# Linear attention and a routed feed-forward layer on one core: constant products beside the keys, products of quarters for the queries, routing in three groups of twelve

## The chip, the cores and the metric

The kernel runs on one core of a Trainium2 chip. The metric is the device time of one execution in microseconds (us). Three runs of the kernel before took 615.9, 616.95 and 619.54 us; their median, 616.95 us, is the time before. All times inside the kernel come from one further execution that the hardware profiler recorded.

The core's engines are TensorE (PE in the profile, with its weight loads as PEld), VectorE (DVE), ScalarE (ACT), GpSimd (POOL) and SyncE (SP, which here only issues DMAs). Each works through its own list of instructions in order and waits for others by semaphores.

## The reference

Eight sequences of 576 tokens with 8 heads of 64 go through linear attention and a norm, and then every one of the 4608 tokens goes through the one expert of eight that it scores highest.

```python
kv = np.einsum('bhsd,bhse->bhde', k, v)
out = np.einsum('bhsd,bhde->bhse', q, kv)
rms = np.sqrt(np.mean(out * out, axis=-1, keepdims=True) + 1e-06)
x = (out / rms * g_norm)            # then rows: 4608 x 512
logits = x @ w_gate
e_idx = np.argmax(logits, axis=1)
gate_w = softmax(logits)[token, e_idx]
eom = 1.0 / (1.0 + np.exp(-(x @ w_output_gate)))
for e in range(8):
    h = np.maximum(x[mask] @ w1[e], 0.0)        # 512 -> 1024
    out[mask] = gate_w * eom[:, e] * (h @ w2[e])  # 1024 -> 512
```

## The kernel before

**Phase one, attention and routing** (`p1_main`, line 837). The loop runs over the 8 sequences, called batches here. For each, `kv_part` (line 460) multiplies keys by values: four chunks of 128 tokens (s = 0 to 3) and a rest of 64 (s = 4), eight products per chunk (line 474; the profile counts two records for each product of 32-bit numbers). ACT copies the sums into `aug` (line 480), DVE into `kvc` (line 482). `kvT_part` (line 485) transposes them and `m_part` (line 494) multiplies them by the gate weights, so that each query row later gives 64 values and 16 gate scores per head.

`out_tile` (line 515) then treats 128 tokens, 36 tiles in all: products of queries with `aug` (line 541, tile `ops`), and three ACT operations that take the result out of PSUM (lines 546, 548, 549). Two PSUM buffers of the tag "big" serve `ops` and the sums of `m_part` in turn. One tile later, DVE adds up the squares (line 562, tile `ss`). During batch b the tiles of batch b-1 are made, the calls of `run_out` (line 797) put them between the steps. Most tiles lie in one batch and multiply 64 rows by 128 tokens at a time; the four tiles across two batches multiply by 64 tokens at a time.

**Routing** (`route`, line 572) is a generator that treats a group of tiles at once with some thirty small DVE operations: the norm's root (lines 589 to 611), the scaling of the gate scores (`gp`, line 618), their sums (`lg`, line 622), the choice of the expert (`ohb`, line 648), a prefix sum on PE (`rps`, lines 676 to 683), the place of each token in its expert's list (lines 689 to 699), one-hot matrices `la` (lines 710 to 723, on the engines that `PLACES` names) and `rrc` (lines 729 to 736), and a table product on PE (`tblps`, line 749). It stops at each `pause`; `advance` (line 787) takes it on to the next one. After the group that ends with tile 23 (`LEAD_GROUP`), the expert with the most tokens so far is known, and its first 384 rows, called the lead here, are worked on before the other tiles are routed.

**The order** in phase one is the program's own (`manual_schedule`, engines in `MAN`): what is written first stands first in each engine's list. `HOOKS` names steps after given tiles and `TAIL` the steps after the last one: R advances the routing, L takes the lead one step on (`lead_run`, line 368: split of the first weights, the three tiles' `stage`, then `mm1`, f = 0 to 7), S splits a chunk of the second weights (`lead_w2`), G gathers the lead's rows, W loads the second weights.

**Slots**: 30 buffers of 4 KB per partition (`SLOTS`) hold loads, rows, weights and so on. `load` (line 448) issues loads as long as more than `SPARE` are free.

**Phase two** (line 1013) runs over nine runs: run 0 is the lead, run 1 the same expert's other rows (320), and then seven experts. `mm1` (line 287) multiplies the rows by the first weights, in eight blocks f of 12 or more products (line 308, tile `hps`, in the two "big" buffers), which ACT and DVE take out (lines 317 and 318, `hT`). `mm2` (line 327) multiplies by the second weights (lines 345 and 350, `yps`), and the rows go out by an indirect DMA (line 361). `stage` (line 255) scales the gathered rows by the norm's root (on DVE or POOL, as `NORMS` says), transposes them on PE (line 271, `tps`) and splits them into a high and a low part on ACT and DVE (lines 276 and 277, `xT`). Weights are split in the same way (`split`, line 198; `whi`, `wlo`). In run 0 the rest of the lead's `mm1`, its three `mm2` and the `stage` steps of run 1 are woven together.

## Time and profile before

| what | value |
|---|---|
| median of three runs | 616.95 us |
| the profiled execution | 620.81 us |
| span of its instructions | 618.8 us |
| TensorE products busy | 566.5 us (92%) |
| DVE, ACT, POOL busy | 263.2, 222.0, 164.0 us |
| granted TensorE clock, mean | 0.931 of full |
| read from and written to memory | 72.63 and 19.99 MB |

The span runs from the first to the last instruction; the execution's 620.81 us contain 2 us more around it. The view by windows gives, for a stretch, the busy time and number of instructions of PE, PEld, DVE, ACT and POOL, then the granted TensorE clock (1.00 is full), the share of the DMA engines in use and the data rate in GB/s. The timeline gives start, length, engine, line, operation, tiles and shapes, and in brackets the idle time before and what ended it; times overlap where an engine is pipelined, so that the distance of two starts is the price of an operation. A shape such as 64*128 64x80 is the part of TensorE's array in use (rows*columns) and the moving operand.

### The profile page before, as it was taken

The page shows a single profiled execution, that of the slowest core. Times are in us where ns is not written, and L with a number is a line of the kernel's source. Part 1 is how long each engine was busy: PE and PEld are TensorE (multiplying, and loading weights), DVE is VectorE, ACT ScalarE, POOL GpSimd, SP SyncE. Part 2 cuts the span into 40 slices and gives each one's busy share as a digit, 9 for nine tenths or more (in the row PEclk, how much of TensorE's full clock was granted, in tenths as well). Part 3 has the DMA queues.
Part 4 walks back from the last instruction along what each step waited for, and adds up shares of the span by engine and source line. Part 5 has one row for each costly group of instructions (what it writes and reads, how often), then busy time and mean ns, then how long its engine had stood idle before and what let it go on. Part 6 is the DMA issues. An engine that isn't in the chain of part 4 may idle for free.

```text
span 618.8 us, 10459 instructions
## 1 busy us (share of the span) xinstructions
PE 566.5 (92%) x4179; PEld 506.3 (82%) x4179; DVE 263.2 (43%) x536; ACT 222.0 (36%) x413; POOL 164.0 (27%) x163
## 2 busy tenths in 40 slices
PE   3799978848999999999899999999999999999991
PEld 3688868747898998889789988998799889889881
DVE  2123688699425456225331453235135325424300
ACT  1335545634225334323331343234234423523310
POOL 2001044443832510630036117104500630110010
PEclk9958777579999999999999999999999999999996
DMA  8999991770564622349776332524432451110010
GB/s 271 367 409 407 405 366 49 246 285 7 166 231 138 202 89 90 87 169 35 16 159 199 115 122 91 172 69 138 145 112 74 135 181 68 53 52 2 0 47 14
DMA packets 39122, 92.53 MB, mean 150 GB/s; under 512 B 14418, under 2 KB 14546, under 8 KB 39072
## 3 DMA queue, kind: packets, MB, share of 16 engines
q1 hardware_dynamic: 32176, 71.63, 37.4%
q0 software_dynamic: 6464, 20.00, 10.2%
q8 instruction: 34, 0.56, 0.4%
q10 hardware_dynamic: 432, 0.21, 0.1%
q14 instruction: 16, 0.13, 0.1%
HBM read 72.63 MB, written 19.99 MB: 150 GB/s over the span
## 4 chain that ended last, share of the span: by engine, by line
PE 57%; issue 19%; DMA 10%; DVE 4%; POOL 3%; ACT 3%; another core or an unknown queue 2%; SPq 0%; POOLq 0%; DVEq 0%
PE hps L308 24%; PE yps L350 23%; PE ops L541 3%; PE kvps L474 3%; DMA ld<-kvm 3%; DMA xs<-xrow 2%; PE tps L271 2%; POOL out L361 2%; DMA ld<-qT 2%; DMA ld<-rem 2%; PE yps L345 1%; POOL xg L239 1%; DMA wraw<-w 1%; DMA xg<-xs,gidx 1%
## 5 line engine op out<-in xcount | busy, mean ns | idle before, releaser
L308 PE MATMUL hps<-xT,whi 128*128 128x320 f32 (+4 forms) x1024 | 197.3, 310 | 9.5 <-DVE hT L318 8.4
L350 PE MATMUL yps<-whi,hT 128*128 128x512 f32 (+2 forms) x592 | 195.9, 399 | 1.0 <-ACT whi L221 1.0
L308 PEld LDWEIGHTS hps<-xT,whi 128*128 128x128 f32 x1024 | 163.6, 191 | 11.9 <-DVE hT L318 9.1
L350 PEld LDWEIGHTS yps<-whi,hT 128*128 128x128 f32 (+2 forms) x592 | 111.3, 188 | 25.2 <-ACT whi L221 1.2
L308 PE MATMUL hps<-xT,wlo 128*128 128x320 f32 (+4 forms) x512 | 121.6, 309 | 0.0
L318 DVE SCALAR_TENSOR_TENSOR hT<-hps,hT 128x512 fp32r<-128x512 f32 (+5 forms) x112 | 59.2, 529 | 142.6 <-ACT hT L317 142.3
L350 PE MATMUL yps<-wlo,hT 128*128 128x512 f32 (+2 forms) x296 | 116.6, 394 | 0.8 <-DVE wlo L224 0.8
L317 ACT ACTIVATE hT<-hps 128x512 fp32r<-128x512 f32 (+5 forms) x112 | 52.5, 469 | 164.0 <-PE hps L308 121.6
L308 PEld LDWEIGHTS hps<-xT,wlo 128*128 128x128 f32 x512 | 89.0, 191 | 0.0
L361 POOL DMA_INDIRECT out<-y,oidx x42 | 44.8, 1068 | 154.2 <-ACT y L360 107.2
L239 POOL DMA_INDIRECT xg<-xs,gidx x42 | 43.2, 1029 | 137.5 <-PE tps L271 54.6
L350 PEld LDWEIGHTS yps<-wlo,hT 128*128 128x128 f32 (+2 forms) x296 | 55.7, 188 | 12.1 <-DVE wlo L224 1.1
L217 DVE SCALAR_TENSOR_TENSOR wlo<-wraw,gcol,whi 128x1024 fp32r<-128x1024 f32 x32 | 43.9, 1372 | 39.6 <-ACT whi L214 39.6
L247 POOL TENSOR_TENSOR xg<-xg 128x512 f32<-128x512 f32 (+3 forms) x40 | 44.0, 1102 | 43.9 <-DMA xg<-xs,gidx 43.5
L541 PE MATMUL ops<-aug,ld 64*128 64x80 f32 (+1 forms) x640 | 49.0, 327 | 5.8 <-ACT gp L549 5.7
L541 PEld LDWEIGHTS ops<-aug,ld 64*128 64x128 f32 (+1 forms) x640 | 44.5, 230 | 8.8 <-ACT gp L549 6.4
L360 ACT ACTIVATE y<-yps,tl 128x512 f32<-128x512 f32 (+2 forms) x37 | 25.5, 689 | 71.4 <-PE yps L350 68.4
L276 ACT CAST xT<-tps 128x512 fp32r<-128x512 f32 (+3 forms) x45 | 23.6, 530 | 67.6 <-PE tps L271 63.9
L277 DVE TENSOR_TENSOR xT<-tps,xT 128x512 fp32r<-128x512 f32 (+3 forms) x45 | 27.7, 617 | 46.9 <-ACT xT L276 43.3
L474 PE MATMUL kvps<-ld 128*64 128x64 f32 (+1 forms) x640 | 36.4, 300 | 11.1 <-DMA ld<-kvm 10.7
L474 PEld LDWEIGHTS kvps<-ld 128*64 128x64 f32 (+1 forms) x640 | 33.1, 209 | 14.0 <-DMA ld<-kvm 12.0
L224 DVE TENSOR_TENSOR wlo<-wraw,whi 128x1024 fp32r<-128x1024 f32 x28 | 34.3, 1226 | 13.5 <-ACT whi L221 6.7
(158 smaller groups left out, 403.2 us busy)
## 6 DMA issues: line engine op xcount, KB each, us to landing
wraw<-w SPq DMA_DIRECT2D x64, 512.0 KB, 3.2
ld<-kvm SPq DMA_DIRECT2D x32, 512.0 KB, 10.2
ld<-qT SPq DMA_DIRECT2D x18, 512.0 KB, 10.2
xs<-xrow SPq DMA_DIRECT2D x13, 512.0 KB, 10.4
xs<-xrow SPq DMA_DIRECT2D x2, 1280.0 KB, 15.2
ld<-rem SPq DMA_DIRECT2D x3, 512.0 KB, 10.2
xg<-xs,gidx POOLq DMA_INDIRECT x42
out<-y,oidx POOLq DMA_INDIRECT x42
```

Source lines behind the costliest of these rows:

```text
L217: eng.scalar_tensor_tensor(out=lo, in0=r, scalar=gcol[:, 0:1], in1=hi.bitcast(F32), op0=ALU.mult, op1=ALU.subtract)
L224: eng.tensor_tensor(out=lo, in0=r, in1=hi.bitcast(F32), op=ALU.subtract)
L239: nc.gpsimd.indirect_dma_start(out=x[:M, :], out_offset=None, in_=rows, in_offset=bass.IndirectOffsetOnAxis(ap=gidx[:M, p, t:t + 1], axis=0))
L247: eng.tensor_tensor(out=v, in0=v, in1=f, op=ALU.mult)
L277: nc.vector.tensor_tensor(out=lo[:, :, c0:c0 + M], in0=v, in1=hi.bitcast(F32)[:, :, c0:c0 + M], op=ALU.subtract)
L308: nc.tensor.matmul(ps[:, j, :n], w[:, o:o + P], x[d][:, j * N:j * N + n], start=(d == 0 and k == 0), stop=(d == 3 and k == 2))
L317: nc.scalar.activation(hh, x, AF.Relu)
L318: nc.vector.scalar_tensor_tensor(out=v(h[:, l:l + n]), in0=x, scalar=0.0, in1=hh.bitcast(F32), op0=ALU.max, op1=ALU.subtract)
L350: nc.tensor.matmul(ps[:M], a, b, start=(f == 0 and k == 0), stop=(f == 7 and k == 2))
L361: i_ = nc.gpsimd.indirect_dma_start(out=out, out_offset=bass.IndirectOffsetOnAxis(ap=oidx[:M, p, t:t + 1], axis=0), in_=y[:M], in_offset=N ...
L474: nc.tensor.matmul(ps[u * D:(u + 1) * D, p * D:(p + 1) * D], k, v, start=(s == 0 and p == 0), stop=(s == 4 and p == NP - 1))
L541: nc.tensor.matmul(ps[r0:r0 + m, u, p * W:(p + 1) * W], qt[g // 2][r, p, q0:q0 + m], augs[b % 3][r, p, :], start=True, stop=True)
```

## The change

**Groups.** `GR` becomes (12, 12, 12): three groups, of which the second ends with tile 23. The first group's gate scores are scaled on DVE (`GPSIMD_GROUPS` 0), its `la` all made on POOL, the second group's on POOL and DVE in turn, the third's on POOL, ACT and DVE in turn. In the second and third group `lg` is summed in two halves (`APART`). Every pause is one stop (`WAITS` is gone).

**Constants.** `constant` multiplies a tile of ones by itself into PSUM that nobody reads, 256 columns for 64 outputs: three products ahead of each of a batch's four chunks, 20 more before the first, and 56 in the tail (step C).

**Steps.** `kv_part` stops before s = 2 and before s = 4, and a tile is made at each stop.

**Quarters.** `out_tile` multiplies 64 rows by 64 tokens in every tile, so that a tile has 16 products instead of 8.

**The lead.** Its rows are scaled on DVE. Its gather and the loads of its weights come after tile 29 instead of after tile 30 and in the tail. In the tail the third group's routing comes first, and the lead's `mm1` and `mm2` (step Y) follow before phase two, whose run 0 now holds only the gather and the `stage` of run 1.

**Slots.** 13 of the 30 are kept for rows (`xfree`), 17 are left for loads; `SPARE` is gone. SP joins the engines whose order is the program's.

```diff
-GR = (10, 10, 4, 12)
+GR = (12, 12, 12)
...
+ROWS = LEAD_TILES // 2 + 1
...
-TAIL = "QLLLLRRRSLSRRSLLRRRLSLRRSRLSLL"
+HOOKS = {25: 'R', 26: 'R', 27: 'R', 28: 'R', 29: 'R', 30: 'RGXW'}
+TAIL = "Q" + 7 * "RC" + "LLLL" + 3 * "RL" + "SLSLSLSLLL" + "YYY"
+COLD = (3, 20)
+GPSIMD_GROUPS = 0
+APART = (1, 2)
...
-NORMS = ("PPP", "VPVP")
-PLACES = ['P', 'P', 'PAV', 'PAV', 'PAV']
+NORMS = ("VVV", "VPVP")
+PLACES = ['P', 'PV', 'PAV']
...
+    def constant(ps, n, start):
+        for _ in range(n):
+            nc.tensor.matmul(ps[0:D, 256:512], ones[:, 0:D], ones.unsqueeze(1).to_broadcast([P, 2, P]), start=start, stop=start)
...
         for s in range(5):
+            if s in (2, 4):
+                yield
+            if s < 4:
+                constant(ps, COLD[0] + (COLD[1] if b == 0 and s == 0 else 0), s == 0)
...
-                for u in range(2):
-                    r = slice(u * D, (u + 1) * D)
-                    nc.tensor.matmul(ps[r0:r0 + m, u, p * W:(p + 1) * W], qt[g // 2][r, p, q0:q0 + m],
-                                     augs[b % 3][r, p, :], start=True, stop=True)
+                for c0 in range(r0, r0 + m, D):
+                    q0 = g % 2 * P + c0
+                    for u in range(2):
+                        r = slice(u * D, (u + 1) * D)
+                        nc.tensor.matmul(ps[c0:c0 + D, u, p * W:(p + 1) * W], qt[g // 2][r, p, q0:q0 + D],
+                                         augs[b % 3][r, p, :], start=True, stop=True)
...
+        elif step == "C":
+            constant(ps_t.tile([P, 512], F32, name="cps", tag="t"), 8, True)
+        elif step == "Y":
+            mm2(0, state["y"], {})
+            state["y"] += 1
...
             if i == 0:
                 gather(1)
                 scale_rows(1)
-                for _ in lead:
-                    next(lead2, None)
-                for _ in lead2:
-                    pass
+                for h in hT[0]:
+                    give(h)
+                for x in range(len(tiles_of(1))):
+                    stage(1, x)
+                continue
```

The first place to see it is TensorE's list in the batch numbered 3 (`aug_117` holds the sums of batch 2, `ld` a load). Before:

```order
L474 MATMUL kvps<-ld 64x64 x40
L541 MATMUL ops<-aug_117,ld 128x80 x8
L489 MATMUL kvTps<-ident,kvc 128x128 x2
L541 MATMUL ops<-aug_117,ld 128x80 x16
L501 MATMUL mps<-gw,kvT 64x16 x8
```

Now, from the second pair of chunks on:

```order
L468 MATMUL kvps<-ones 64x256
L488 MATMUL kvps<-ld 64x64 x8
L556 MATMUL ops<-aug_117,ld 64x80 x16
L488 MATMUL kvps<-ld 64x64 x8
L556 MATMUL ops<-aug_117,ld 64x80 x16
L503 MATMUL kvTps<-ident,kvc 128x128 x2
```

The keys' products stand in pieces between tiles, the constants ahead of them, and each tile has twice the products of half the width. The second place is TensorE's list behind the last tile (`tps`: the lead's transposes, `hps`: its first products, `tblps`: the third group's table). Before:

```order
L541 MATMUL ops<-aug_116,ld 128x80 x32
L271 MATMUL tps<-ident,xg 128x128 x12
L308 MATMUL hps<-xT,whi 128x384 x2
L308 MATMUL hps<-xT,wlo 128x384
L308 MATMUL hps<-xT,whi 128x384 x2
```

Now, after the last of the third group's prefix products:

```order
L697 MATMUL rps<-ohb_118,triu 128x104
L468 LDWEIGHTS ones
L468 MATMUL cps<-ones 64x256
...
L274 MATMUL tps<-ident,xg 128x128 x12
L763 LDWEIGHTS la
L763 MATMUL tblps<-rrc,la 128x96
...
L311 MATMUL hps<-xT,whi 128x384 x2
```

The lead's first products used to follow its transposes at once; now the third group's prefix products stand before the transposes, and its table product between them and `hps`. The third place is DVE's list from the last sums of squares on. Before:

```order
L562 TENSOR_REDUCE ss<-sq 128x8 x3
L267 COPY tl<-xg 128x1
L277 TENSOR_TENSOR xT<-tps,xT 128x2x128 x2
...
L217 SCALAR_TENSOR_TENSOR wlo<-wraw,gcol,whi 128x1024
L589 TENSOR_SCALAR ra<-ss 128x96
...
L618 TENSOR_TENSOR gp<-gp,xtail 128x1536
L318 SCALAR_TENSOR_TENSOR hT<-hps,hT 128x384
```

Now:

```order
L577 TENSOR_REDUCE ss<-sq 128x8 x7
L603 TENSOR_SCALAR ra<-ss 128x96
...
L687 TENSOR_SCALAR rogs<-rogs 128x12
L219 TENSOR_SCALAR whi<-wraw,gcol 128x1024
L220 SCALAR_TENSOR_TENSOR wlo<-wraw,gcol,whi 128x1024
L250 TENSOR_TENSOR xg<-xg 128x512
L270 COPY tl<-xg 128x1
L280 TENSOR_TENSOR xT<-tps,xT 128x2x128 x2
...
L703 TENSOR_TENSOR rw<-rps,ohb_118 128x96
```

The routing of the third group up to `rogs` has moved ahead of the lead's first weights and rows, and the rest of it, from `rw` on, stands directly behind them and ahead of the lead's first `hT`.

More of the change, by code (lines that the diff above doesn't have):

```diff
@@ L165, in body, with take @@
     ps_y = main.enter_context(tc.tile_pool(name="ps_y", bufs=1, space=psum))
[L166 removed]
+    free = list(range(SLOTS - ROWS))
+    xfree = list(range(SLOTS - ROWS, SLOTS))
     held = {}
[L169 removed]
+    def take(shape, dt, name, free=free):
         i = free.pop(0)
@@ L332, in mm2 @@
         T = half(i)
-        ps = ps_y.tile([P, DM], F32, name="yps", tag=f"y{ny % 2}")
-        ny += 1
+        if i == 0:
+            ps = ps_b.tile([P, 2, 512], F32, name="yps0", tag="big")[:, 0]
+        else:
+            ps = ps_y.tile([P, DM], F32, name="yps", tag=f"y{ny % 2}")
+            ny += 1
         tl = tails.pop((p, t))
@@ L352, in mm2 @@
                 e()
-        y = hp.tile([P, DM], F32, name="y", bufs=3)
+        y = take([P, DM], F32, "y0") if i == 0 else hp.tile([P, DM], F32, name="y", bufs=3)
         if M == T:
@@ L446, in body, with load @@
                 nq += 1
-    def load(spare):
-        while loads and len(free) > spare:
+    def load():
+        while loads and free:
             where, k, src = loads.pop(0)
@@ L804, in run_out @@
             advance()
-            load(SPARE)
+            load()
             if not loads and not opened[0]:
                 open_rows(0)
-            if lead_placed and opened[0] and (0, 1, 0) not in raw and (1, 0) not in wgt:
-                for c in range(1):
-                    wload(0, 1, c)
             for step in HOOKS.get(done_tiles, ""):
@@ L855, in p1_main @@
             advance()
+        for _ in lead:
+            assert False
+        for _ in lead2:
+            assert False
     vec = nc.vector
```

59 lines of the change are left out of this document (26 added, 33 removed).

## The prediction

> **What bounds the kernel now.** I read the page first, then the busy times by windows, then the timelines of PE and DVE from the first loads to the second run.
>
> ```profile
> span 618.8 us, 10459 instructions
> 28.00:48.00 20.00, 16.95 (x228) 15.31 (x230) 3.76 (x6) 8.23 (x21) 0.00 (x0) 0.50 1.03 409
> 48.00:84.00 36.00, 32.14 (x612) 29.45 (x610) 20.25 (x59) 18.50 (x51) 8.87 (x11) 0.80 1.03 402
> 84.00:118.00 34.00, 28.25 (x400) 26.07 (x393) 29.86 (x97) 18.88 (x52) 13.91 (x19) 0.68 0.55 170
> 118.00:175.00 57.00, 44.29 (x222) 38.14 (x221) 39.29 (x90) 19.80 (x40) 29.89 (x26) 0.86 0.53 173
> 174.69 0.45 PE L308 MATMUL hps<-xT,whi 128*128 128x320 f32 x2
> 161.93 5.48 PE yps L350 x24
> ```
>
> Up to 84 us the loads run at full rate (DMA share 1.03, some 405 GB/s), but PE is behind them, at 0.50 to 0.80 of its clock. From 84 to 118 us the DMA share halves and DVE is the fullest engine (29.86 of 34 us): it routes. From 118 to 175 us PE has 57 us for the lead. The first product of run 1 starts at 174.69; from there on the order of work is the same in both kernels, and PE works nearly without a gap. So what the change is worth is how far 174.69 moves. I split the time before it at two marks: A, DVE's copy `kvc` of batch 6, and B, the end of the last tile's products.
>
> ```profile
> 28.69 1.12 PE L474 MATMUL kvps<-ld 128*64 128x64 f32 x16 [0.73 <-DMA ld<-kvm]
> 60.66 0.42 DVE L482 COPY kvc<-kvps 128x256 f32<-128x256 f32 x1 [4.27 <-ACT aug L480]
> 84.14 0.42 DVE L482 COPY kvc<-kvps 128x256 f32<-128x256 f32 x1 [1.88 <-ACT aug L480]
> 109.02 8.65 PE L541 MATMUL ops<-aug,ld 64*64 64x80 f32 x96
> 137.04 1.01 PE L308 MATMUL hps<-xT,whi 128*128 128x384 f32 x2 [7.76 <-DVE hT L318]
> ```
>
> A is at 84.14, B at 109.02 + 8.65 = 117.67. Between B and run 1 lie 57.0 us; one stall of 7.76 us in them is PE waiting for DVE, which had the routing in front of `hT`.
>
> **Up to A: quarters, steps, constants, slots.** The rows for prices at half and at full clock:
>
> ```profile
> 35.62 1.30 PE L541 MATMUL ops<-aug,ld 64*64 64x80 f32 x30
> 83.52 0.72 PE L541 MATMUL ops<-aug,ld 64*64 64x80 f32 x30
> 46.15 3.81 PE L474 MATMUL kvps<-ld 128*64 128x64 f32 x80
> 95.53 4.58 PE L474 MATMUL kvps<-ld 128*64 128x64 f32 x80
> 112.00:116.00 4.00, 4.00 (x40) 3.81 (x38) 2.74 (x4) 2.74 (x7) 3.36 (x5) 0.50 0.70 190
> 124.00 0.84 PE L308 MATMUL hps<-xT,whi 128*128 128x384 f32 x2
> 124.96 0.84 PE L308 MATMUL hps<-xT,whi 128*128 128x384 f32 x2
> 127.53 0.52 PE L308 MATMUL hps<-xT,whi 128*128 128x384 f32 x2
> 128.07 0.52 PE L308 MATMUL hps<-xT,whi 128*128 128x384 f32 x2
> 77.06 6.50 POOL L719 TENSOR_SCALAR la<-ni,rlon 128x128 bf16<-128x128 f32 x10 [18.75 <-DVE rlon L698]
> ```
>
> Quarters are in the trace: the tiles across two batches have them. Such a tile (32 records, 30 of them in the row) costs 1.4 us cold and 0.8 warm. The 8.65 us hold one such tile and four of the other kind, all cold: (8.65 - 1.4) / 4 = 1.8 each. The gain is 0.4 us for each of 32 tiles when cold, some 13 us of PE time.
>
> A constant product has no row. The nearest: three products of 384 columns take 0.96 us cold and 0.54 warm, so 0.32 and 0.18 each, and 256 columns 0.21 and 0.12. Where PE would wait for keys it costs nothing; below nothing it can go by the clock. Twelve in a batch are 2.6 us cold, 1.4 warm.
>
> A batch's 80 records of keys cost 4.6 us cold; the 3.81 us were half warm, so I put 3.0 warm. Four and a half tiles are 6.3 or 3.6. Now four batches (46.15 to 95.53) take 12.3 us each; after keys (4.2) and tiles (6.4 or more) some 1.7 us are left for transposes, gate sums and gaps, and these stay. So a batch will cost 9.7 us warm, 15.2 cold; its loads (28.3 MB over eight, at 409 GB/s) cost 8.65. PE stays behind the loads either way; with only 17 slots ahead the loads may fall back to PE's pace, but that pace sets the time already.
>
> The clock: 112 to 116 us are solid `ops` products at 0.50, while 2 to 4 us of keys raise it (0.50 to 1.00 within the row at 46.15). With constants a pair of chunks is a stretch of 3.1 us of such work, so I expect more warm time, not all. The Trainium skill, page "TensorE: Matmul & The Clock Gate", section "Why this matters for your kernels", says to keep TensorE busy for at least 4 us to reach the full clock. The row at 112 us disagrees: busy throughout, and half the clock. By that rule everything up to B would be warm, which is the first rival's case.
>
> From 28.69 (set by loads), two batches and the first 6.5 to 10 us of a third lead to batch 4's `kvc`: 55 warm, 69 cold; now it is at 60.66. I take 57. From there another wait decides. By the prices of the next part DVE needs 5.8 us to the first group's `ohb` (with the copy, two `ss`, a whole `lg`, `mx` and on), 3.3 more to `rlon`; then POOL makes twelve `la`, at 0.65 us each (6.50 for 10) 7.8 us; and in PE's list the table product that needs the last of them stands ahead of batch 5's gate sums, hence of batch 6. That is 57 + 16.9 = 73.9. Then table and gate sums, 1.1 us, and the constants, keys and two tiles of batch 6, 6.5 (warm) to 10.5 (cold); I take 8, and 0.4 for ACT's copy: **A = 83.4, that is -0.7 us** (-6 to +6). What quarters and clock win is mostly lost to POOL.
>
> **From A to B: two routings become one of twelve tiles.** Rows of the group of twelve that exists now:
>
> ```profile
> 84.48 0.67 DVE L562 TENSOR_REDUCE ss<-sq 128x8 f32<-128x512 f32 x1
> 104.54 0.16 DVE L867 TENSOR_TENSOR cnt<-rps,cf 128x8 f32<-128x8 f32 x1
> 105.99 0.15 DVE L879 CAST epos<-eposf 128x1 int32<-128x1 f32 x1
> 128.26 0.21 DVE L592 TENSOR_SCALAR ry<-ra 128x96 int32<-128x96 int32 x1
> 129.38 0.26 DVE L605 SCALAR_TENSOR_TENSOR ry<-ru,ry 128x96 f32<-128x96 f32 x1
> 134.76 1.76 DVE L618 TENSOR_TENSOR gp<-gp,xtail 128x1536 f32<-128x1536 f32 x1
> 138.09 2.80 DVE L622 TENSOR_REDUCE lg<-gp 128x192 f32<-128x1536 f32 x1
> 140.93 0.25 DVE L632 TENSOR_REDUCE mx<-lg 128x12 f32<-128x96 f32 x1
> 142.09 0.26 DVE L648 TENSOR_TENSOR ohb<-rsc,rsx 128x96 bf16<-128x96 f32 x1
> 144.39 0.25 DVE L668 TENSOR_TENSOR rog<-ohb,lg 128x96 f32<-128x96 bf16 x1
> 146.12 0.16 DVE L704 TENSOR_TENSOR cnt<-rps,cf 128x8 f32<-128x8 f32 x1
> 147.72 0.75 DVE L729 TENSOR_TENSOR rrc<-cf,rhk 128x576 bf16<-128x576 f32 x1
> 149.76 0.29 DVE L740 RECIPROCAL rdn<-rdn 128x24 f32<-128x24 f32 x1
> ```
>
> From A, DVE's list holds without a wait: `kvc` 0.4; five `ss` at 0.6, 3.0; nine root steps at 0.28 (three steps from 128.26 to 129.10 and so on), 2.6; `gp` 1.8; half of `lg` 1.4; `mx` to `ohb` 1.3; totals 0.4; the other half 1.4; `rog` to `cnt` 1.7; the lead's choice 1.5; six `la` on DVE 1.2; `rrc` to the reciprocal 2.1. Sum 18.8. PE's list has the group's table product ahead of batch 7's last keys, so tiles 29 to 35 wait for it; nothing covers that. The table takes 0.6, seven tiles 9.8 cold (PE has been idle) or 5.6 warm, and the steps between them, keys, copies, transposes, gate sums, an estimated 3.2. Sum 32.4 instead of 117.67 - 84.14 = 33.5: **-1.1 us** (-4 to +1).
>
> **From B to run 1: the lead behind the routing.**
>
> ```profile
> 114.06 0.92 DVE L216 TENSOR_SCALAR whi<-wraw,gcol 128x1024 fp32r<-128x1024 f32 x1
> 124.63 1.28 DVE L217 SCALAR_TENSOR_TENSOR wlo<-wraw,gcol,whi 128x1024 fp32r<-128x1024 f32 x1 [0.62 <-ACT whi L214]
> 158.01 0.69 DVE L247 TENSOR_TENSOR xg<-xg 128x512 f32<-128x512 f32 x1 [1.66 <-DMA xg<-xs,gidx]
> 121.19 1.08 PE L271 MATMUL tps<-ident,xg 128*128 128x128 f32 x4 [1.62 <-DVE xT L277]
> 123.58 0.42 DVE L277 TENSOR_TENSOR xT<-tps,xT 128x256 fp32r<-128x256 f32 x1 [0.44 <-ACT xT L276]
> ```
>
> Before the lead's first product now come, one after the other: the last tile's squares, 1.8 (three operations of ACT at 2.74 / 7, and one `ss`); the root steps, `gp`, half `lg`, `ohb`, half `lg`, `rog` to `rogs`, 2.6 + 1.8 + 1.4 + 1.3 + 1.4 + 0.7 = 9.2; the first weights' split 0.92 + 1.28 = 2.2; three tiles of rows, each scaled on DVE (0.65), then transposed cold and copied out (121.19 to 123.58 + 0.42, 2.8) with DVE waiting, 10.3 in all or 8.8 with warm transposes, I take 9.5; `rw` to the last `la`, 149.76 - 144.39 less those 0.7, 4.7; the table 0.5. Sum 27.9; now the second of the first block's four steps starts at 124.00, so the first some 5 us behind B. The 56 constants of the tail (12 us cold) lie in that wait and cost nothing. The moved gather (POOL) and the eight weight loads (SP, now ahead of the late rows) are issued some 23 us behind A by these sums, and are wanted 45 us behind it: not late.
>
> Then `mm1`: eight blocks of four steps at 0.53, 17.0, plus 1.9 for a cold first 4 us, plus an estimated 1 us where DVE's `wlo` stands before an `hT`: 19.9. `mm2`: 3 x 5.48 = 16.4. Last, run 1's `stage`, which used to lie under `mm2`: two transposes, DVE's `xT` twice, the scaling of the third tile, its transpose and copies, an estimated 4.2 from eight steps of 0.4 to 0.7 one behind the other. Sum 68.4 against 57.0: **+11.4 us** (+7 to +18).
>
> **The sum.** -0.7 - 1.1 + 11.4 = +9.6 us. The profiled execution would take 620.8 + 9.6 = 630.4; it lies 3.9 above the median of the runs, so on that scale 616.95 + 9.6 = **626.5 us**. About 0.5%, 3.1 us, is what a measurement of this kernel can tell from no change.
>
> **Rivals.**
> 1. *The constants keep the clock full; not slower.* Place: the keys of batches 3 to 7. Then `kvc` of batch 4 is at 55 and A at 79.7; A to B 18.8 + 0.6 + 5.6 + 3.2 = 28.2; B to run 1 loses the cold parts (0.7 and 1.9), 65.8. Run 1 starts at 173.7, -1.0 us: 616, and 613 if the estimated 1 us and some of the gaps go too. It decides once B falls before 109. For it: 3.1 us stretches of full columns. Against it: 40% of a batch stays `ops`, which did not hold the clock at 112 us. It is what the rule of the Trainium skill above would do.
> 2. *The constants do not raise the clock and only cost.* At today's clock a batch is 12.3 - 1.6 + 2.0 = 12.7 us; `kvc` of batch 4 at 62, A at 90: +6 there, and 633 us. For it: a constant fills half the columns. Against it: the row at 46.15.
> 3. *DVE holds up the lead's products as it does now.* The 7.76 us stall recurs once behind POOL's weight splits, +7: 633 us. Against it: the routing is out of DVE's list by then.
>
> **Chances.** Forecast 0.50; rival 1 0.25, of which 0.09 lie over 0.5% below and 0.16 within; rival 2 0.15; rival 3 0.10. So faster 0.09, same 0.16, slower 0.75. Range 614 to 636: from rival 1's better half to rival 2 with its bounds.
>
> **What would show it.** Right: `kvc` of batch 6 near 83, a wait of PE for `la` at the first group's table, the last `ops` 32 us after A, then some 28 us with little but constants on PE before `hps`, and 4 us idle ahead of run 1. Wrong: the clock at 1.00 from 30 to 90 us with A below 80, or `hps` within 20 us of B; then the DVE sums are too long and the kernel is not slower.

## The result, and the profile after

| | before | after |
|---|---|---|
| median of four runs | 617.65 us (615.9 to 619.54) | 636.91 us (634.51 to 641.19) |
| the profiled execution | 620.81 us | 634.51 us |
| its span | 618.8 us | 632.7 us |

The change makes the kernel slower: the ratio of the times is 1.0319, with a 95% interval from 1.0252 to 1.0385. The forecast was 626.5 us with a range up to 636, so the direction is right and the size is not: 636.91 lies just above the range. Between the two profiled executions the loss is 13.7 us; between the medians it is 19.3, because the profiled execution of before lies 3.2 above that kernel's median and that of after 2.4 below its own. The ratios leave out executions that are more than 1.5% above the fastest of the same kernel.

In the new kernel DVE's timeline shows `kvc` of batch 4, which was forecast at 57, and A, `kvc` of batch 6, forecast at 83.4:

```profile
64.32 0.42 DVE L496 COPY kvc<-kvps 128x256 f32<-128x256 f32 x1 [0.98 <-ACT aug L494]
91.86 0.42 DVE L496 COPY kvc<-kvps 128x256 f32<-128x256 f32 x1 [2.44 <-ACT aug L494]
```

PE's timeline of the new kernel has the last `ops` (its end, 121.64, is B), two waits for the third group's routing, the first `hps`, and the `stage` in front of run 1:

```profile
120.86 0.78 PE L556 MATMUL ops<-aug,ld 64*64 64x80 f32 x32 [0.37 <-ACT gp L564]
...
130.99 0.50 PE L695 MATMUL rps<-ohb,ones 128*128 128x96 bf16 x12 [3.79 <-DVE ohb L662]
...
149.93 1.12 PE L763 MATMUL tblps<-rrc,la 128*128 128x96 bf16 x12 [6.05 <-DVE rrc L750]
150.83 0.99 PE L311 MATMUL hps<-xT,whi 128*128 128x384 f32 x2
...
189.72 0.43 PE L274 MATMUL tps<-ident,xg 64*128 64x64 f32 x4 [3.80 <-issue]
190.61 1.10 PE L311 MATMUL hps<-xT,whi 128*128 128x320 f32 x2 [0.46 <-ACT xT L279]
```

Run 1 starts at 190.61 instead of 174.69. By the marks of the prediction:

| stretch | before | forecast | after |
|---|---|---|---|
| up to A | 84.14 | 83.4 | 91.86 |
| A to B | 33.5 | 32.4 | 29.8 |
| B to first `hps` | 5.1 | 27.9 | 29.2 |
| first `hps` to run 1 | 51.9 | 40.5 | 39.8 |
| run 1 to the end of the span | 444.1 | unchanged | 442.1 |

Everything behind A came within 3 us of its forecast. A came 8.5 us late, and that is the miss. A is not the same point of the work in both kernels, though: by ACT's copies out of PSUM 22 tiles are done at A before and 25 after, since the steps put tiles ahead of `kvc`. Tile 25 was out at 89.2 us before and at 93.0 after, the last tile at 119.0 and 123.1. So against the kernel before the front lost 4 us; against the forecast, which counted those tiles in, it is 8.5 at A and 5.8 at B (121.64 for 83.4 + 32.4). The next two fences show the stretch from `kvc` of batch 2 to A, batch by batch, from one `kvc` to the next. Columns: length, then busy time and count of PE, PEld, DVE, ACT and POOL, clock, DMA share, GB/s. Before:

```profile
36.30:50.40 14.10, 13.31 (x190) 12.28 (x182) 3.76 (x6) 6.99 (x18) 0.00 (x0) 0.56 1.03 409
50.40:60.66 10.26, 9.23 (x190) 8.38 (x187) 4.91 (x15) 5.55 (x15) 2.37 (x1) 0.83 1.02 407
60.66:73.68 13.02, 11.47 (x190) 10.54 (x184) 7.74 (x19) 6.89 (x18) 0.00 (x0) 0.74 1.03 407
73.68:84.14 10.46, 9.19 (x190) 8.34 (x186) 7.60 (x27) 5.79 (x17) 6.50 (x10) 0.84 1.04 389
```

After:

```profile
37.95:51.54 13.59, 10.45 (x270) 9.50 (x270) 3.74 (x6) 6.89 (x19) 0.00 (x0) 0.75 1.03 408
51.54:64.32 12.78, 10.22 (x238) 9.22 (x238) 6.86 (x16) 5.56 (x16) 0.00 (x0) 0.73 1.03 398
64.32:76.93 12.61, 10.37 (x284) 9.31 (x284) 9.26 (x22) 7.15 (x21) 2.00 (x4) 0.86 0.85 292
76.93:91.86 14.93, 11.27 (x250) 9.74 (x250) 5.40 (x13) 5.64 (x16) 5.34 (x9) 0.77 1.03 363
```

PE's busy time in the four batches went from 43.2 to 42.3 us, its idle time from 4.6 to 11.6 (53.91 less 42.31). So PE did not become busier; it stands still more. What it waits for from 28 to 92 us, by the view of waits of the new kernel:

```profile
PE kvTps L503 <- DVE kvc L496: 5.7, 5, 1.3
PE mps L515 <- issue: 2.9, 2, 2.1
PE ops L556 <- issue: 2.2, 2, 1.5
PE tblps L763 <- DVE rrc L750: 1.3, 1, 1.3
PE tblps L763 <- POOL la L733: 1.3, 4, 0.4
```

New against before are 5.7 us in which the transposes wait for `kvc`, 2.6 us for the first group's table (before, 3.6 us for `rps`), and 5.1 us of "issue", where PE stands still in the middle of a tile or of the gate sums and the view of waits names nothing that it waits for.

The DMA view does: what PE lacks there are its instructions. The pages of before and after list a DMA queue for instructions, in packets, MB and share of the DMA engines:

```profile
q8 instruction: 34, 0.56, 0.4%
q8 instruction: 39, 0.64, 0.4%
```

That is packets of some 16 KB, and by its count the queue is PE's: one packet for 242 to 249 records of PE and PEld in each of the twenty traces. One of the stalls in PE's timeline of the new kernel:

```profile
39.41 0.41 PE L515 MATMUL mps<-gw,kvT 64*64 64x16 f32 x14
41.87 0.29 PE L515 MATMUL mps<-gw,kvT 64*64 64x16 f32 x2 [2.05 <-issue]
```

Read in windows of 0.25 us, the DMA view has an instruction packet at 33.0, 39.25, 52.0 and 64.5 us, and PE's four "issue" stalls in the new kernel end at 35.56, 41.87, 54.63 and 67.01. In all traces together there are 49 such stalls from 14 to 92 us, and each ends 2.3 to 2.8 us behind a packet. From 26.75 to 64.5 us the new kernel's packets are 6.25 to 6.5 us apart, the kernel before's from 28 to 82 us 7.5 to 10.5. Quarters double the tiles' instructions, and beside the full loads PE gets no more of them than that; where the loads thinned for a while (DMA share 0.41 to 0.75 from 67 to 70 us), the next packet came after 4.25 us.

### The profile page after: what moved, and what is told of

Read it like the earlier page. It is cut to its first block, busy times and chain, and to the rows that moved or that the text cites. A ratio compares the mean times of both kernels' runs of the same rounds, so it can differ in the third digit from the quotient of the medians.

```text
span 632.7 us, 11778 instructions
## 1 busy us (share of the span) xinstructions
PE 563.1 (89%) x4860; PEld 503.5 (80%) x4860; DVE 258.3 (41%) x510; ACT 220.8 (35%) x409; POOL 154.1 (24%) x155
## 4 chain that ended last, share of the span: by engine, by line
PE 58%; issue 20%; DMA 7%; DVE 5%; POOL 5%; ACT 3%; POOLq 0%; ACTq 0%; SPq 0%; DVEq 0%
PE hps L311 26%; PE yps L356 20%; PE ops L556 3%; DMA wraw<-w 3%; PE tps L274 2%; PE kvps L488 2%; POOL out L367 2%; DMA ld<-qT 2%; PE kvps L468 2%; DMA wgs<-wg 1%; PE yps L351 1%; POOL la L733 1%; ACT sq L563 1%; POOL xg L242 1%; DMA out<-y,oidx 1%
## 5 line engine op out<-in xcount | busy, mean ns | idle before, releaser
L356 PE MATMUL yps<-whi,hT 128*128 128x512 f32 (+2 forms) x592 | 193.8, 396 | 0.0
L242 POOL DMA_INDIRECT xg<-xs,gidx x42 | 41.9, 998 | 131.3 <-PE tps L274 51.9
L250 POOL TENSOR_TENSOR xg<-xg 128x512 f32<-128x512 f32 (+3 forms) x37 | 39.4, 1068 | 47.6 <-DMA xg<-xs,gidx 34.4
L488 PE MATMUL kvps<-ld 128*64 128x64 f32 (+1 forms) x640 | 41.2, 262 | 3.1 <-DMA ld<-kvm 2.6
L733 POOL TENSOR_SCALAR la<-ni,rlon 128x128 bf16<-128x128 f32 x22 | 14.1, 652 | 118.2 <-DVE rlon L712 118.2
L556 PE MATMUL ops<-aug,ld 64*64 64x80 f32 x1152 | 34.4, 258 | 8.6 <-ACT gp L564 3.7
L577 DVE TENSOR_REDUCE ss<-sq 128x8 f32<-128x512 f32 x36 | 24.4, 682 | 37.0 <-ACT sq L563 37.0
## 6 DMA issues: line engine op xcount, KB each, us to landing
ld<-qT SPq DMA_DIRECT2D x18, 512.0 KB, 10.4
```

The lines of the kernel that those rows point to most:

```text
L242: nc.gpsimd.indirect_dma_start(out=x[:M, :], out_offset=None, in_=rows, in_offset=bass.IndirectOffsetOnAxis(ap=gidx[:M, p, t:t + 1], axis=0))
L250: eng.tensor_tensor(out=v, in0=v, in1=f, op=ALU.mult)
L356: nc.tensor.matmul(ps[:M], a, b, start=(f == 0 and k == 0), stop=(f == 7 and k == 2))
L488: nc.tensor.matmul(ps[u * D:(u + 1) * D, p * D:(p + 1) * D], k, v, start=(s == 0 and p == 0), stop=(s == 4 and p == NP - 1))
L556: nc.tensor.matmul(ps[c0:c0 + D, u, p * W:(p + 1) * W], qt[g // 2][r, p, q0:q0 + D], augs[b % 3][r, p, :], start=True, stop=True)
```

## The experiments

Ratios are to the kernel before on the same chip. B to run 1 is read from each trace as above.

| kernel | median, us | ratio, 95% interval | A | B | first `hps` | run 1 |
|---|---|---|---|---|---|---|
| before | 617.65 | | 84.14 | 117.67 | 122.74 | 174.69 |
| after | 636.91 | 1.0319 (1.0252 to 1.0385) | 91.86 | 121.64 | 150.83 | 190.61 |
| no_steps | 638.67 | 1.0369 (1.0303 to 1.0435) | 91.34 | 123.23 | 152.40 | 193.59 |
| no_key_consts | 630.83 | 1.0233 (1.0178 to 1.0287) | 85.95 | 115.86 | 145.05 | 185.19 |
| whole_tiles | 637.23 | 1.0367 (1.0288 to 1.0446) | 86.36 | 120.78 | 149.79 | 190.26 |
| whole_no_consts | 638.66 | 1.0349 (1.0287 to 1.0411) | 90.79 | 126.33 | 155.32 | 196.46 |
| front_plain | 636.18 | 1.0264 (1.0240 to 1.0288) | 84.03 | 120.02 | 149.04 | 188.86 |
| places_pav | 638.68 | 1.0330 (1.0301 to 1.0359) | 91.05 | 124.10 | 153.24 | 194.33 |
| lead_first | 636.06 | 1.0310 (1.0256 to 1.0365) | 91.22 | 122.18 | 135.28 | 192.35 |
| lead_as_before | 634.47 | 1.0247 (1.0215 to 1.0279) | 92.52 | 125.87 | 131.76 | 193.08 |
| stage_under | 635.76 | 1.0295 (1.0248 to 1.0341) | 93.74 | 127.10 | 156.13 | 194.36 |
| no_tail_consts | 635.20 | 1.0299 (1.0247 to 1.0351) | 91.42 | 122.22 | 151.35 | 191.73 |
| tail_all | 626.63 | 1.0141 (1.0082 to 1.0201) | 92.14 | 121.92 | 128.06 | 180.47 |
| front_tail | 624.40 | 1.0063 (1.0039 to 1.0088) | 85.30 | 121.28 | 126.23 | 178.48 |
| quarters_alone | 618.17 | 1.0011 (0.9984 to 1.0037) | 81.52 | 115.06 | 119.53 | 171.37 |
| consts_alone | 625.23 | no interval | 82.78 | 115.64 | 120.47 | 172.20 |
| consts_again | 620.68 | 0.9992 (0.9948 to 1.0035) | 86.00 | 119.10 | 123.74 | 175.57 |
| row_list | 613.40 | 0.9928 (0.9901 to 0.9955) | 84.22 | 117.98 | 122.89 | 174.85 |
| row_list_av | 611.03 | 0.9868 (0.9842 to 0.9895) | 83.82 | 117.27 | 122.17 | 170.86 |
| late_quarters | 610.64 | 0.9885 (0.9846 to 0.9923) | 81.21 | 111.28 | 119.10 | 168.07 |

Six of these kernels (after, lead_first, lead_as_before, stage_under, no_tail_consts, tail_all) are the same up to A, and have it at 91.2 to 93.7. Four others are the same as before up to A (before, row_list, row_list_av, late_quarters): 81.2 to 84.2. So A says something where it differs by more than 3 us. B is less sure: those first six have the same code up to tile 34, and B at 121.6 to 127.1. By A, 24 or 25 tiles are out of PSUM in the kernels with steps and 22 in those without (all from before's side, and no_steps, front_plain and front_tail), so across these two groups A compares different amounts of work.

### What holds up batches 3 to 6

My first theory was the steps. **no_steps** writes a batch's keys in one piece again.

```diff
-            if s in (2, 4):
-                yield
...
-            for _ in range(2):
-                next(kv)
-                load()
-                run_out(lim)
             cp = next(kv)
...
             kvT = kvT_part(cp)
             run_out(lim)
+            run_out(lim)
```

> The changed kernel without the steps: all keys of a batch in one piece, then one tile behind the copy of the sums (kvc), two behind the transposes (kvTps), as in the kernel before; constants, quarters, slots and groups stay. Theory 1 (the steps took away the tiles that covered the chain keys - kvc - kvTps - kvT - mps, so that PE stands idle some 3.5 us in each batch and then runs at half clock): the batches fall from 12.7 to 10.5-11 us, kvc of batch 6 comes at 85-87 instead of 91.86, and the time falls by 4 to 6 us, to some 631. Theory 2 (the constants' own time and PE's stalls for instructions make the batch 12.7 us): batches stay at 12.5 or more, kvc of batch 6 at 91 or later, the time within 1.5 us of the changed kernel's 636.9.

A at 91.34 (with 22 tiles out for 25), the time not better: the theory fell. The wait for `kvc` shrank, and others grew in its place.

**no_key_consts**:

```diff
-COLD = (3, 20)
+COLD = (0, 0)
```

> The changed kernel without the constants among the keys (the number in front of each chunk and at the start set to 0); the rest stays, the tail's constants too. Theory 1 (steps): the constants cost 1.4 to 2.6 us of PE in a batch but hold the clock in part; without them the clock falls, the batches stay at 12 to 13 us, and the time stays within 2 us of 636.9. Theory 2 (the constants are the loss): batches fall to 10.5-11 us, kvc of batch 6 to 84-86, the time to 630 or less.

A at 85.95, B at 115.86, 6 us less in the median. From `kvc` of batch 2 to A, and the longest wait from 14 to 92 us:

```profile
34.77:85.95 51.18, 35.80 (x1016) 30.98 (x1016) 25.07 (x56) 25.15 (x68) 7.70 (x12) 0.87 1.02 394
```

```profile
PE ops L556 <- issue: 10.6, 6, 2.4
```

PE has 6.5 us less to do (35.80 for 42.32) at a higher clock than with the constants (0.87 for 0.78), and the stretch is only 2.7 us shorter: PE idles 15.4 us of it. Its instruction packets come 6.0 to 6.75 us apart up to 84 us. So beside quarters and steps the constants are a net loss, the one edit whose removal alone pays.

**whole_tiles** takes the quarters out, the loop over `c0` in `out_tile` becoming one pass over all rows of a part as before.

> The changed kernel with tiles in halves of the array, as before the change; the rest stays. Theory 1 (PE waits in a chain whose length the tile does not set, as long as it is shorter than the wait): longer tiles (1.1 for 0.8 us warm, 1.8 for 1.4 cold) fill PE's idle time, batches 12.5 to 13.3 us, and only the seven tiles from kvc of batch 6 on cost 2 to 3 us; the time is 638 to 641. Theory 2 (PE's own work sets the batch): 4.5 tiles of 0.3 to 0.4 more each, batches 14.2 us, kvc of batch 6 at 97 or later, and the time 643 or more.

```profile
38.77:86.36 47.59, 41.75 (x788) 37.38 (x786) 24.96 (x57) 25.33 (x68) 7.46 (x12) 0.93 1.03 403
```

Here the clock was 0.93 and PE idle only 5.8 us; A came at 86.36. The "issue" stalls are gone. But from A to B whole tiles cost 34.4 us instead of 29.8 (29.8 to 33.4 in the six traces above), and run 1 starts where it did. In the changed kernel quarters lose some 5 us beside the loads and win about as much behind them.

**quarters_alone** and **consts_alone** put one edit each into the kernel before (the loop over `c0`; three constants per chunk and twenty at the start).

> The kernel before with the quarters alone (each tile of queries in 32 products of 64 rows instead of 16 of 128). Theory 1 (quarters double PE's instructions, and PE then stands still without any wait shown, 2 to 10 us in the first 92 us; whole tiles showed none): PE saves 0.3 to 0.4 us of work in a tile but idles as 'issue' for 4 to 10 us up to the last tile; kvc of batch 6 comes at 83 to 87 (84.14 without), the time 615 to 620. Theory 2 (the stalls come with constants and steps): no 'issue' stalls of 0.5 us or more, kvc of batch 6 at 80 or earlier, the last tile ends 4 to 8 us earlier, the time 610 to 613.

> The kernel before with the constants alone (three in front of each chunk of keys, twenty more at the start). Theory 1 (they add 1.4 to 2.6 us of PE time to a batch and raise the clock, from 0.50 between 28 and 48 us to 0.8 or more, so that the two cancel): kvc of batch 6 at 82 to 86, the time 616 to 620. Theory 2 (they only cost): the clock there stays at 0.6 or less, kvc of batch 6 at 88 or later, the time 621 or more. Theory 3 (the first rival of the prediction: they keep the clock full and win): kvc of batch 6 at 80 or earlier, the time 613 or less.

Quarters alone, `kvc` of batch 2 to A, and two lines of the waits from 14 to 92 us:

```profile
34.36:81.52 47.16, 35.25 (x998) 31.46 (x990) 24.17 (x65) 25.42 (x68) 8.86 (x11) 0.78 1.03 405
```

```profile
PE ops L541 <- ACT gp L549: 6.7, 6, 1.9
PE ops L541 <- issue: 6.4, 3, 3.0
```

Constants alone:

```profile
34.48:82.78 48.30, 42.89 (x778) 39.52 (x772) 24.05 (x65) 25.12 (x68) 8.87 (x11) 0.86 1.03 405
```

In the kernel before, the stretch takes 47.84 us at a clock of 0.73. Quarters take 7.9 us of work from PE and it takes 47.16: PE waits for ACT to empty the PSUM buffers, and for instructions, whose packets come 6.0 to 7.0 us apart from 20 to 90 us. With constants the clock is 0.86 and it takes 48.30: their own products take up what the clock gives (PE is busy 42.89 us, 43.2 before). Neither moved the time. A higher clock alone does shorten this stretch: late_quarters, whose code is the kernel before's up to A, happened to have 0.81 in it and took 44.76 us. consts_alone left two of four executions near 620 us and two near 630, so it was timed again as **consts_again**:

> The same kernel as consts_alone. Theory 1 (the two executions at 629-630 were the constants' doing, one in two or so): the times spread from 620 to 630 again, while the kernel before stays within 3 us. Theory 2 (chance, nothing to do with the constants): all within 3 us of one another, and within 2 us of the kernel before.

Twelve executions from 611.7 to 630.1 us, median 620.68 against 618.06, ratio 0.9992 (0.9948 to 1.0035): no gain, and a spread more than twice that of before (613.7 to 621.2). In its trace the stretch took 49.99 us at a clock of 0.83. Why the times spread stays open.

**whole_no_consts** and **front_plain** remove two and all three of the front's edits.

> The changed kernel without the constants among the keys and with whole tiles; steps, slots, groups and tail stay. Theory 1 (constants cost PE time and quarters stall it, each about 5 us up to kvc of batch 6): no 'issue' stalls, batches 11.5 to 12.3 us as before the change, kvc of batch 6 at 82 to 85, but the last tiles cost 4 us more than in quarters (34 us from there to the last product), so run 1 starts at 185 to 188 and the time is 629 to 633. Theory 2 (the two overlap: what one leaves, the other takes): kvc of batch 6 at 85.5 or later, the time 632 or more.

> The changed kernel with whole tiles, no constants among the keys and no steps: of the change, the two pools of slots, the groups of twelve and the tail are left. Theory 1 (constants, quarters and steps together are what makes batches 3 to 6 slow): batches as before the change (10.3 to 13 us), kvc of batch 6 at 83 to 86, from there 33 to 35 us to the last product, and with the tail as it is the time is 630 to 634. Theory 2 (the slots: the loads run at 270 to 300 GB/s from 65 to 80 us because 17 slots are given back late, and PE gets its keys late): kvc of batch 6 at 89 or later, the time 636 or more.

```profile
35.82:84.03 48.21, 40.15 (x744) 35.71 (x738) 25.14 (x56) 25.14 (x68) 7.32 (x12) 0.82 1.03 403
```

With all three gone A is at 84.03, as before the change and with 22 tiles out as there; the pools of slots are not the cause. With the steps left in and the other two gone it is 90.79, two tiles more, with PE busy 46.09 us at 0.76, and B comes 6.3 us later than in front_plain: the steps seem to cost there, which they did not in no_steps. The three edits interact, and I can't split the 8 us among them. And at B only 1.6 us of the 8 are left (120.02 for 121.64), in part because three tiles fewer are done at A, in part because whole tiles are slower behind it. Run 1 starts 1.75 us earlier, and the ratio falls from 1.0319 to 1.0264, inside the interval of the former; theory 1 had the time at 630 to 634 us. So the front's three edits together cost this kernel little.

**places_pav** spreads the first group's `la` over POOL, ACT and DVE:

```diff
-PLACES = ['P', 'PV', 'PAV']
+PLACES = ['PAV', 'PV', 'PAV']
```

> The changed kernel with the twelve la of the first group on POOL, ACT and DVE in turn instead of all on POOL, as it has them in the third group; all else stays. Theory 1 (the first group's table waits for POOL and PE's gate sums of batch 5 with it; this delays batch 6 by 4 us): the table comes at 77 to 79 instead of 79.9 to 82.6, no wait for POOL in it, kvc of batch 6 at 87 to 89, the last product 2 to 4 us earlier, the time 632 to 635. Theory 2 (the table waits for DVE's rrc as long, and PE's stalls and waits then fill the gap): kvc of batch 6 at 91 or later, the time within 1.5 us of 636.9.

```profile
81.62 1.12 PE L763 MATMUL tblps<-rrc,la 128*128 128x96 bf16 x12 [0.21 <-DVE rrc L750]
```

The wait for POOL is gone from the table, but the table waits for DVE instead and ends at 82.74 us, as it did (82.59), and A is at 91.05, within the spread. The wait was real and cost nothing that another did not take.

### From the last tile to run 1

**lead_first** gives the tail nearly the order of before, without its constants; **lead_as_before** also scales the lead's rows on POOL and splits its first weights at tile 34.

```diff
-TAIL = "Q" + 7 * "RC" + "LLLL" + 3 * "RL" + "SLSLSLSLLL" + "YYY"
+TAIL = "QLLLLRRRSLSRRSLLRRRLSLLRRLSLL" + "YYY"
```

> The changed kernel with the order of its tail as before the change: the lead's weights, rows and products stand ahead of and among the third group's routing, which has the last tile's sums ahead of it; no constants in the tail. Theory 1 (the order of the tail is the 12 us from the last tile's products to run 1: the lead's products wait for 18 us of DVE's routing with nothing beside it): the first hps comes 5 to 12 us behind the last ops instead of 29, DVE's routing lies beside 18 us of products, from B to run 1 some 55 to 61 us instead of 69, and the time falls by 8 to 14 us, to 623-629. Theory 2 (the stretch is set by DVE's work as a whole, and the products then wait for hT behind the routing): the hps have stalls of 7 us or more in them, and the time falls by less than 5 us.

> The changed kernel with the lead's inputs where they were before the change: its rows scaled on POOL and its first weights split at tile 34, its rows and products ahead of and among the third group's routing, no constants in the tail. The order alone (lead_first) moved the first hps from 29 to 13 us behind the last ops and gave nothing, with 9.6 us of waiting for ohb and 6 us ahead of run 1. Theory 1 (scaling and splitting on DVE behind the last sums is what the order alone left: it delays the lead's rows and the routing both): the first hps comes 6 to 8 us behind the last ops, from B to run 1 60 to 64 us instead of 69 to 70, the time 627 to 631. Theory 2 (DVE's list for the twelve tiles behind the last product, with its steps slowed beside POOL, sets the stretch whatever stands first): the wait for ohb or hT grows by what hps gains, from B to run 1 67 us or more, the time 634 or more.

PE's timeline in lead_first:

```profile
135.28 1.15 PE L311 MATMUL hps<-xT,whi 128*128 128x384 f32 x2 [0.46 <-ACT xT L279]
...
151.10 0.70 PE L695 MATMUL rps<-ohb,ones 128*128 128x96 bf16 x12 [9.60 <-DVE ohb L662]
...
160.99 0.62 PE L311 MATMUL hps<-xT,whi 128*128 128x384 f32 x2 [3.00 <-DVE hT L321]
```

and in lead_as_before:

```profile
146.12 1.01 PE L311 MATMUL hps<-xT,whi 128*128 128x384 f32 x2 [7.75 <-DVE hT L321]
...
161.04 1.01 PE L311 MATMUL hps<-xT,whi 128*128 128x384 f32 x2 [5.97 <-DVE hT L321]
```

The first `hps` moved 16 and 23 us nearer to B, and B to run 1 stayed at 70.2 and 67.2 us. The prediction's third rival, DVE holding up the lead's products, appears as soon as the order lets it: 12.6 and 13.7 us of waits for DVE, 9.6 of them at `rps`, which stands among the products.

**stage_under** puts run 1's `stage` back under `mm2` of run 0 (no "YYY", no `continue` ahead of the loop over `mm2`).

> The changed kernel with run 1's rows transposed (its stage) under the second products of the lead again, as before the change, and with those products behind the gather of run 1's rows; all else stays. Theory 1 (the stage in the open costs 6 us: three tiles one behind the other): the gap of 6.4 us between the lead's last product and run 1 falls below 1.5 us, from B to run 1 63 to 65 us instead of 69, the time 630 to 633. Theory 2 (the gather or DVE's scaling is what is late, and moves the wait into the products): gaps of 3 us or more in or behind the products, the time within 2 us of 636.9.

```profile
176.31 0.50 PE L356 MATMUL yps<-whi,hT 128*128 128x512 f32 x1 [2.27 <-DVE hT L321]
...
194.36 0.45 PE L311 MATMUL hps<-xT,whi 128*128 128x320 f32 x2
```

The gap in front of run 1 went, and 2.27 us of waiting and the stage's transposes came into the products: 67.3 us. **no_tail_consts** (`7 * "R"` in the tail) has 69.5:

> The changed kernel without the 56 constants among the third group's routing. Theory 1 (they lie in PE's wait for DVE and cost nothing, nor do they keep the clock, since the waits behind them are long): from B to run 1 68 to 70 us, the time within 2 us of the changed kernel. Theory 2 (they warm PE for the transposes or products behind them): transposes and the first products cost 1.5 to 3 us more without them.

So the tail's constants cost nothing that shows, as the prediction had it. **tail_all** undoes the order, the scaling and the stage together, and takes POOL's weight splits from beside DVE's routing:

```diff
-SPLITS = ['VV', 'AV', 'AV', 'AV', 'AP', 'AP', 'AP', 'AP']
+SPLITS = ['VV', 'AV', 'AV', 'AV', 'AV', 'AV', 'AV', 'AP']
```

> The changed kernel with all of its tail undone: the lead's rows on POOL and its first weights at tile 34, its products among the routing, run 1's rows under the lead's second products; and besides, three wlo of the second weights on DVE instead of POOL (worth 3 to 4 us in the kernel before: row_list_av). The front stays as the change has it. Theory 1 (from the last product to run 1 the change lost 12 us to three things at once, each of which hides the others: the lead's inputs late, DVE's steps slowed beside POOL, the stage in the open): the first hps 6 to 8 us behind the last ops, waits for hT of 5 us or less in sum, no gap ahead of run 1, from B to run 1 54 to 59 us, the time 621 to 627. Theory 2 (groups of twelve leave DVE too much behind the last product, however it is ordered): from B to run 1 63 us or more, the time 630 or more.

```profile
128.06 1.15 PE L311 MATMUL hps<-xT,whi 128*128 128x384 f32 x2 [0.46 <-ACT xT L279]
...
180.47 0.45 PE L311 MATMUL hps<-xT,whi 128*128 128x320 f32 x2
```

B to run 1 is 58.5 us, 10.4 less, and the ratio falls from 1.0319 to 1.0141. Each part that was tried alone gave 2 us or nothing, since the next one then waited. Some 3.3 of the 10.4 may be the splits', which the change had not touched: in the kernel before they shorten the stretch from 56.9 to 53.6 us (row_list and row_list_av). **front_tail** joins this with front_plain:

> front_plain and tail_all in one: of the change, only the two pools of slots, three groups of twelve instead of 10, 10, 4 and 12, and the lead of 24 tiles' rows are left, with three wlo on DVE besides. Theory 1 (slots and groups cost nothing by themselves): kvc of batch 6 at 83 to 86, from there 33 to 35 us, then 54 to 59 us to run 1, which starts at 171 to 179; the time is 612 to 620. Theory 2 (the groups or slots carry a part of the loss): run 1 at 181 or later, the time 623 or more.

1.0063, or 3.9 us above the kernel before, and the splits' gain is in it, which the kernel before does not have. Against row_list_av below, which has the same splits, run 1 starts 7.6 us later (178.48 for 170.86), about half of it by B. So what is left of the change, the groups with their places and stops and the slots, costs some 4 to 7 us; which of them it is was not tried. That is theory 2 by the time, though run 1 came earlier than its 181.

### A version that beats both

**row_list** edits the kernel before alone. Its list of overflow rows goes to memory as every other value of a tile; in two tiles the values are neighbours.

```diff
-        met = sm.tile([P, NOVER, 2], F32, name="met")
+        met = [sm.tile([P, NOVER], F32, name=f"met{i}") for i in range(2)]
...
-        nc.sync.dma_start(out=tab, in_=met[:, :, 0])
+        nc.sync.dma_start(out=tab, in_=met[0])
```

> The kernel before with one edit of its own: the list of overflow rows is made in two tiles instead of one with two columns, so that its transfer to memory reads 44 neighbouring values of a row and not every other one. Theory 1 (that transfer moves 1 GB/s from 284 to 300 us and holds up the weights behind it, whose late arrival leaves PE idle 2.3 us at 300 to 308 us and at half clock for 3 us more; the change moved it to where it hides): the share of the DMA engines stays below 0.6 there, PE has no gap, and the time falls by 2 to 4 us, to 613-616. Theory 2 (the weights come late for another reason): the gap at 300 to 308 us stays, the time within 1 us of 617.

The DMA view from 276 to 312 us, packets and the time of a weight load to landing; before:

```profile
DMA packets 5885, 0.92 MB, mean 26 GB/s; under 512 B 5669, under 2 KB 5669, under 8 KB 5883
...
wraw<-w SPq DMA_DIRECT2D x5, 512.0 KB, 26.6
```

and row_list:

```profile
DMA packets 1054, 3.31 MB, mean 92 GB/s; under 512 B 260, under 2 KB 260, under 8 KB 1051
...
wraw<-w SPq DMA_DIRECT2D x5, 512.0 KB, 3.1
```

The weights no longer wait behind 5600 small packets; run 1 to the end takes 439.25 us instead of 444.1. In the changed kernel the same list goes out at 298.7 us and PE has no gap there, which I take to be its 2 us behind run 1; this was not tried by itself.

**row_list_av** adds the `SPLITS` of tail_all. **late_quarters** adds quarters from the 31st tile on (`step = D if g >= 30 else m`).

> The kernel before with the overflow list in two tiles (as in row_list, 613.4 us) and with the low parts (wlo) of three of the lead's second weights made on DVE instead of POOL. Theory 1 (DVE's steps of 0.2 us take 2.4 us while POOL makes a wlo beside them, three of them ahead of hT, some 6.5 us; three wlo on DVE cost 3.8 us): the wait of hps for hT falls from 7.7 us to 3-5.5, run 1 starts 2 to 4 us earlier, the time 609.5 to 611.5. Theory 2 (the slow steps are not POOL's doing, or the three wlo stand in the way as long): steps of 2.4 us stay, or hps wait for DVE as long in sum; the time 613 or more.

> The kernel before with the overflow list in two tiles and three wlo on DVE (row_list_av, 611.0 us), and quarters for the tiles from the 31st on alone, where the loads are over. Theory 1 (quarters stall PE only beside the loads; behind them they save 0.4 us in each cold tile of two halves): the last six tiles end 1.5 to 2.5 us earlier, no 'issue' stalls, run 1 starts 1 to 2.5 us earlier, the time 608.5 to 610.5. Theory 2 (what PE saves there, DVE's sums or the lead's rows take): the last product comes earlier and run 1 does not, the time within 0.7 us of 611.

Two rows of DVE in the kernel before, and POOL's `wlo` beside the first:

```profile
129.68 2.44 DVE L607 SCALAR_TENSOR_TENSOR ru<-ry 128x96 f32<-128x96 f32 x1
132.16 2.28 DVE L609 TENSOR_TENSOR ru<-ru,ra 128x96 f32<-128x96 f32 x1
```

```profile
129.66 4.66 POOL L224 TENSOR_TENSOR wlo<-wraw,whi 128x1024 fp32r<-128x1024 f32 x2 [1.50 <-ACT whi L221]
```

The same two in row_list_av:

```profile
126.92 0.26 DVE L607 SCALAR_TENSOR_TENSOR ru<-ry 128x96 f32<-128x96 f32 x1
127.21 0.26 DVE L609 TENSOR_TENSOR ru<-ru,ra 128x96 f32<-128x96 f32 x1
```

Run 1 starts 4.0 us earlier than in row_list, and row_list_av takes 611.03 us, ratio 0.9868: faster than both kernels. late_quarters (0.9885) can't be told from it; its trace has run 1 another 2.8 us earlier, but 2.6 of them were there at A already, where the code is the same. From A to B it takes 30.1 us for 33.5, so behind the loads quarters do save; from B to run 1 it then takes 56.8 for 53.6.

## Why the prediction was wrong, point by point

- **Up to A: wrong.** The step that failed is the batch price, "after keys and tiles some 1.7 us are left for transposes, gate sums and gaps, and these stay", and with it "`kvc` of batch 4 ... I take 57". It came at 64.32, 7.3 late; from there to A it was 27.5 us for a forecast 26.4, so the rest of that chain held. I summed PE's work and took the gaps as they were; that PE's instructions reach it in time was a term that I put at nothing. In its place the trace shows the packets 6.25 to 6.5 us apart from 26.75 to 64.5 us, with 265 to 269 of PE's records each; for `kvc` at 57 they would have had to come every 5 us (an estimate, 30 us over the same six). From `kvc` of batch 2 to that of batch 4 the kernel took 26.4 us, for which 57 leaves some 21 by my prices: in each of the two batches 10.3 us of work where I had some 9, since the clock was 0.73 to 0.75 and I had counted on nearly full, and 2.9 us of gaps for 1.7. A higher clock did not shorten the stretch either: lead_first, the same code up to A, had 0.87 for 0.78 and PE 2.9 us less busy, and from batch 2 to A it took 53.07 us for 53.91.
- **POOL's la hold the first group's table: right as a wait, but it does not set A.** The table ended at 82.59, 18.3 us after `kvc` of batch 4 (forecast 17.5). Without that wait (places_pav) A stays.
- **A to B: right within the spread,** 29.8 for 32.4: here the tiles ran at full clock, where I put them cold, 0.78 us each in the row at 120.86; stage_under, the same code up to B, took 33.4.
- **B to run 1: right,** +11.9 for +11.4, and its parts too. What the sum did not show is that undoing the order alone gives nothing back.
- **The scale.** I moved the sum from the profiled execution to the medians; the two executions differ by 13.7, the medians by 19.3. By the marks the spans differ by 7.7 - 3.7 + 11.9 - 2.0 = 13.9. So of the 10.4 us between 626.5 and 636.91 the marks hold 4.3 (13.9 for 9.6); 0.7 are the median of before, and 5.4 lie between the profiled executions and the medians. Part of those may be the front, since the other five traces with the same code up to tile 34 have B 0.3 to 5.5 us later than this one; the rest no trace locates.
- **Rivals.** The first (clock full, not slower) did not happen: A at 91.86, not 79.7. The second had the numbers of the front nearly right (batches 12.7, batch 4 at 62, A at 90, 633 us) for half a reason: the constants do cost, but consts_alone, consts_again and whole_tiles have the clock higher (0.86, 0.83 and 0.93; four traces of the kernel before's code have 0.72 to 0.81), and what it gave went into the constants' own products and into waiting. The rule that I set beside the first rival, from the Trainium skill, page "TensorE: Matmul & The Clock Gate", section "Why this matters for your kernels" (keep TensorE busy and get the full clock), was nearly met in whole_tiles, and run 1 came at 190.26 all the same.

## What to carry to other kernels

Where an engine that is behind also has gaps, price the gaps as a chain of their own, one operation behind the other across the engines, and ask whether less work or a higher clock shortens that chain; here 7.9 us less work on TensorE moved nothing. Count instructions as well as work: the edit that saved those 7.9 us doubled the tiles' products, and beside full loads the instructions came too slowly. When a change has several parts, undo them together as well as one by one: the parts of the tail gave 2 us or nothing each, and 10 with the splits together. Look for transfers of single values and for GpSimd beside VectorE's small steps first: those two edits gave 1.3%.
